# Linear and softmax attention on one core: projections as column tiles, zero products in planned idle time, delayed fills, smaller GpSimd groups

## The chip, the core and the metric

One NeuronCore of a Trainium2 chip runs the whole program. Its engines work side by side and wait for each other through semaphores: TensorE (PE, with its weight loads shown as PEld) multiplies matrices into PSUM, ScalarE (ACT) computes exponentials, VectorE (DVE) does elementwise work and empties PSUM, GpSimd (POOL) does elementwise work between SBUF buffers, and SyncE (SP) issues transfers. Each engine executes its own instructions strictly in the order in which the program lists them. The metric is the device time of one execution in microseconds (us); the time before is the median of three runs.

## The reference

Two attention blocks, A and B, have the same sizes: one sequence of S = 2048 rows, D = 512, H = 32 heads of 16. A is a linear attention, B a full softmax attention. The results are put side by side.

```python
qkv = (x @ wqkv).reshape(B, S, 3, H, Dh).transpose(2, 0, 3, 1, 4)
q, k, v = qkv[0], qkv[1], qkv[2]
# A
phi = lambda t: jnp.where(t > 0, t + 1, jnp.exp(t)) + 1e-6
pq, pk = phi(q), phi(k)
kv = jnp.einsum("bhsd,bhse->bhde", pk, v)
z = jnp.einsum("bhsd->bhd", pk)
o = einsum("bhqd,bhde->bhqe", pq, kv) / (einsum("bhqd,bhd->bhq", pq, z)[..., None] + 1e-6)
# B
scores = jnp.einsum("bhqd,bhkd->bhqk", q, k) * Dh ** -0.5
o = jnp.einsum("bhqk,bhkd->bhqd", softmax(scores), v)
# both
o.transpose(0, 2, 1, 3).reshape(B, S, D) @ wo
```

Nearly all the work is B's: 32 x 2048 x 2048 exponentials. Inputs and outputs are bfloat16.

## The kernel before, in words

**Blocks and units.** B's score matrix is cut into 32 units of 64 blocks. A unit is four heads (one in each group of 32 rows of PE) and 512 queries; a block is 128 keys by 512 queries of one head. `qk` (line 733) makes the scores of a block: K = 32 rows of PE, so up to four blocks of different row groups can run at once. `pv_cand` (line 982) multiplies the exponentials of a block by 17 columns (16 of V and a column of ones) in one of four column groups of PE, and the 48 or more products of a head accumulate in one PSUM bank, `pPV`. When a unit ends, `unit_done` (line 1007) lets DVE transpose that bank, divide, and store into `ON`.

**Two ways to an exponential.** Five PSUM banks (`pS`) form two slots of three and two banks. `fill_act_cand` fills a slot with three or two blocks and ACT computes the exponentials of the whole slot in one operation (line 889). The two `pD` banks serve the other way: DVE turns scores into 16-bit integers whose bits are an approximate exponential in float16 (`DI`, line 829, one block at a time), and GpSimd makes two shifted copies (`DJ`, line 936); the three versions are multiplied by V scaled with three weights, so such a "D block" takes three PV products. A fill may carry D blocks in row groups that its own blocks leave free (`d_pick`, `d_take`, `d_emit`), or `fill_d_cand` makes them alone. D blocks are gathered into groups of `DG` = 3, in `NDG` = 4 group buffers; GpSimd starts on a group when its last block is there (`chain`). `DBL` and `PBL` bound the planned backlog of DVE and GpSimd.

**Projections and block A.** These are jobs of up to 16 products that share the two `pD` banks: `proj_job` (Q and K of B, line 491), `v4_job` (V of B, line 553), `akv_job` (K and V of A, line 590), `aq_job` (Q of A, line 624), `omm_job` (both output projections, line 677), and small ones. `halves` cuts the products of a job into `NPP` = 4 parts, and other work can stand between the parts; the bank stays taken until DVE has emptied it. The products use the full 128 x 128 array. The phi of A takes ACT (line 578) and two bfloat16 operations of DVE (lines 579 and 581).

**The order.** The program is written out by a planner, a loop that keeps a planned clock `T` for each engine. In each step it collects candidates with a planned start and length, drops PE candidates that would let ACT run dry (`keep`), and emits the one that starts first, by priority within 0.03 us. The planned durations are constants: 0.22 us for a fill and for a PV round, 0.216 us for a product of 512 columns, 0.09 + 0.51 us for the integer step of a D block, 0.05 us plus 0.000833 us a column for an exponential. `switch(kind)` adds 0.1 us when PE changes between score products ("q"), PV products ("v") and full-array products ("f"). What the planner fixes is only the order on each engine; on the chip the semaphores decide when an instruction starts.

```python
start = max(T["pe"], t0, afree[sl], ptfree.get((row, sl), 0.0) - 0.5)
dur = switch("q") + 0.22
...
bi = min((i for i in range(ND) if dfree[i] is not None), key=lambda i: (dfree[i], i), default=None)
...
if bi is None or u is None or dfree[bi] > at or d_backlog(at) > DBL or p_backlog(at) > PBL or lagging(at):
    return None
```

The first two lines are of the fill for ACT, the others of `d_pick`: a fill takes a D block along only if a `pD` bank is free when the fill starts.

Of the kernel before, what the change touches and what calls it, by code (L numbers as in the profile page):

```python
# [7 lines left out]
BF = mybir.dt.bfloat16  # L8
# [226 lines left out]
def bass_concat_heads__linear_attn_block__softmax_full_mha__prompt_kernel(nc, A_x, A_wqkv, A_wo, B_x, B_wqkv, B_wo, out):  # L235
# [22 lines left out]
    DBL = 4.0  # L258
    PBL = 4.5
    SHL = ("pool", "pool")  # L260
    TRACE = None


# [7 lines left out]
    with es:  # L271
# [151 lines left out]
        tok = {}  # L423
        seq = [0]

        def push(eng, ready, prio, dur, run):
            seq[0] += 1
            cands[eng].append((ready, prio, seq[0], dur, run))

        class Job:  # L430

# [12 lines left out]
            def stage_done(self, i, end, bk, bi):  # L444
                eng = self.stages[i][0]
                if i == self.rel and bi is not None:
                    dfree[bi] = vis(eng, end)
                for st, tk in self.gives:
                    if st == i:
                        tok[tk] = vis(eng, end)  # L450
                if i + 1 < len(self.stages):
                    eng2, dur, fn = self.stages[i + 1]
                    push(eng2, end if eng2 == eng else vis(eng, end),
                         self.prio if eng2 == "pe" else (0 if eng2 == "act" or (i + 1 <= self.rel and self.bank) else min(self.prio, 2)), dur,
                         lambda st_, en_, fn=fn: (fn(bk), self.stage_done(i + 1, en_, bk, bi)))
# [16 lines left out]
        def halves(fn, reads, n=4, parts=NPP, dur=MM, after=None):  # L472

            def mk(lo, hi):
                def f(e, bk):
                    for i in range(lo, hi):
                        ins = fn(e, bk, i)
                    return ins
                def add(bk):
                    sch.add("pe", lambda e: f(e, bk), reads=reads, writes=[bk[3]], accum=("ch", bk[3], id(fn)))  # L480
                    if after is not None and hi == n:
                        after()
                return add
            w = n // parts
            return [("pe", w * dur, mk(i * w, (i + 1) * w)) for i in range(parts)]
# [2 lines left out]

        def proj_job(Gp, sc, kind, fast=False, **kw):
            def mm(e, bk, cc):  # L490
                return e.matmul(f32v(bk), lhsT=Wb[:, cc, kind * 512 + Gp * 128:kind * 512 + Gp * 128 + 128],  # L491
                                rhs=xTb[:, cc, sc * 512:(sc + 1) * 512], start=(cc == 0), stop=(cc == 3))
            r = Gp % 2
            cs = slice(sc * 512, (sc + 1) * 512)
            i = Gp * NC + sc
            st = halves(mm, [("Wb", kind, Gp)] + [("xTb", t) for t in range(4 * sc, 4 * sc + 4)])
# [87 lines left out]
        def akv_job(t, hp, **kw):  # L584
            n = 4 * hp + t // 4
            c0 = (n % 2) * 512 + (t % 4) * 128
            def mm(e, bk, i):
                k_, cc = divmod(i, 4)
                o_ = f32v(bk)[:, 128:384] if k_ == 0 else f32v(bk).rearrange("p (a n) -> p a n", n=128)[:, 0::3, :]
                return e.matmul(o_, lhsT=xTa[:, cc, c0:c0 + 128],  # L590
                                rhs=Wa[:, cc, 512 + 512 * k_ + 256 * hp:512 + 512 * k_ + 256 * hp + 256], start=(cc == 0), stop=(cc == 3))
# [28 lines left out]
        def aq_job(sc, bq, **kw):  # L620
            n = 8 + sc
            c0 = (n % 2) * 512
            def mm(e, bk, cc):
                return e.matmul(f32v(bk), lhsT=Wa[:, cc, bq * 128:(bq + 1) * 128], rhs=xTa[:, cc, c0:c0 + 512],  # L624
                                start=(cc == 0), stop=(cc == 3))
            st = halves(mm, ["Wa", ("xTa", n % 2)], after=(lambda: next_xa(n)) if bq == 3 else None)
# [46 lines left out]
        def omm_job(ab, t, o2, needs, gives, lane="dve", **kw):  # L673
            WO, wkey, col0 = (WOa, "WaV", 0) if ab == "a" else (WOb, ("Wb", 2), 512)
            def mm(e, bk, hb):
                src = ONT[:, t % 2, hb * 128:(hb + 1) * 128] if ab == "a" else ON[:, 4 * hb + t // 4, (t % 4) * 128:(t % 4 + 1) * 128]
                return e.matmul(f32v(bk), lhsT=src, rhs=WO[:, hb, :], start=(hb == 0), stop=(hb == 3))  # L677
# [5 lines left out]
            return Job(halves(mm, ins_ + [wkey]) + [(lane, 0.6 if lane == "dve" else 0.48, fin)],  # L683
                       needs + [("akv", 1, bl) for bl in range(2)], gives, **kw)


# [156 lines left out]
        def fill_act_cand():  # L843
# [53 lines left out]
        def fill_d_cand():  # L897
# [7 lines left out]
            at = max(at, T["pe"] + d_backlog(T["pe"]) - DBL + 0.01)  # L905
            pk = d_pick(at + 1e-6, ())
            if pk is None:
                return None
# [184 lines left out]
        def job_cand():  # L1093
            best = None
            bi = min((i for i in range(ND) if dfree[i] is not None), key=lambda i: dfree[i], default=None)
            for lst, pr in ((urgent, 0.5), (early, 2), (bjobs, 2.2), (urgent2, 2.3), (ajobs, 2.5)):
                for pos, j_ in enumerate(lst[:1] if lst is not urgent2 else lst[:8]):
# [9 lines left out]
                    if best is None or (st, pr) < (best[0], best[1]):  # L1107
                        def run(st_, en_, j_=j_, lst=lst, fn=fn):
# [6 lines left out]
                        best = (st, pr, eng, dur, run)  # L1115
            return best

        npick = 0
        while True:
            opts = []  # L1120
            for eng in T:
# [5 lines left out]
                        best = (k_, st, c_)  # L1127
                if best is not None:
                    c_ = best[2]
                    opts.append((best[1], c_[1], eng, c_[3] + (switch("f") if eng == "pe" else 0.0), c_[4], c_, "f"))  # L1130
            fa = fill_act_cand()
            if fa is not None:
                opts.append((fa[0], 0, "pe", fa[1], fa[2], None, "q"))
# [7 lines left out]
                opts.append((pc[0], pc[3], "pe", pc[1], pc[2], None, "v"))  # L1141
            jc = job_cand()
            if jc is not None:
                opts.append((jc[0], jc[1], jc[2], jc[3] + (switch("f") if jc[2] == "pe" else 0.0), jc[4], None, "f"))
            if not opts:
                break

# [11 lines left out]
            if eng == "pe":  # L1159
                pk[0] = kind  # L1160
            run_(st, st + dur)
            npick += 1
            if TRACE is not None:
# [3 lines left out]
        if TRACE is not None:  # L1167
            for w in range(0, int(max(T.values())) + 1, 50):
                print(w, {k_: round(sum(max(0, min(b_, w + 50) - max(a_, w)) for a_, b_, e_, _ in TRACE if e_ == k_), 1) for k_ in T}, dgroup["n"])
            print("plan", {k_: round(v_, 1) for k_, v_ in T.items()}, npick,  # L1170
                  {k_: round(sum(b_ - a_ for a_, b_, e_, _ in TRACE if e_ == k_), 1) for k_ in T})

        last = {}
# [77 lines left out]
```

## Time and profile before

| | us |
|---|---|
| runs | 810.81, 813.84, 801.38 (median 810.81) |
| the profiled execution, its time | 817.54 |
| its span, first to last instruction | 815.8 |
| mean granted clock of PE | 0.916 of full speed |

The profile comes from one execution, so durations in the prediction are set against 815.8 us and 817.54 us. A page of it lists the busy time of each engine, a strip of 40 slices of the span, the chain of work that ended last, and the costliest groups of instructions by line. In a group row, "x640 | 738.6, 1349" means 640 instructions, 738.6 us in which at least one of them ran, 1349 ns as the mean of one; what follows is the idle time of the engine just before them and what ended it. Instructions overlap in their pipelines, above all on PE, so a mean is longer than the distance from one to the next. PEclk is the clock that was granted to PE, in tenths of full speed.

Of the chain that ended last, ACT holds 62%, PE 23% and DVE 13%; 60% of the span is the exponential at line 889.

### The profile page before, as it was taken

Reading aid. Unit: us, or ns where it says so; the run is one execution under the profiler, and the core shown is the slowest. Engines: PE = TensorE matmul, PEld = TensorE weight load, DVE = VectorE, ACT = ScalarE, POOL = GpSimd, SP = SyncE. Lnnn points to the kernel's source line nnn. Section 1 sums busy time; section 2 is a strip of 40 time slices with the busy share of each in tenths; the row PEclk is TensorE's granted clock in tenths of the full one; section 3 lists DMA queues with packets and bytes.
Section 4 is the critical chain, followed back from the end, with each engine's and each line's share of the span. In section 5 each row is a group of like instructions: output and inputs, shape, how many; then the busy total and the mean of one; then the engine's idle time right before and its main releaser. Section 6 shows DMA issues by size and latency. Waiting matters only on the chain.

```text
span 815.8 us, 14322 instructions
## 1 busy us (share of the span) xinstructions
PE 726.8 (89%) x6056; PEld 214.7 (26%) x6056; DVE 536.9 (66%) x829; ACT 751.7 (92%) x677; POOL 467.3 (57%) x349
## 2 busy tenths in 40 slices
PE   7989899999988898988999899899888998998986
PEld 4222332222222332322222232222222222222221
DVE  4865766775786666688467666787676556647361
ACT  4989999999998998999988999999998899999894
POOL 3386764554667474546555766545765555639370
PEclk9978999999997998999876999999998689889797
DMA  9400101101101102011001101001100000100000
GB/s 198 113 2 1 27 1 33 40 8 27 28 1 27 27 2 59 7 35 33 14 7 15 26 20 47 7 12 28 27 8 1 7 14 33 33 27 2 10 17 29
DMA packets 54486, 21.43 MB, mean 26 GB/s; under 512 B 45200, under 2 KB 53904, under 8 KB 54416
## 3 DMA queue, kind: packets, MB, share of 16 engines
q1 hardware_dynamic: 53360, 20.20, 11.1%
q8 instruction: 49, 0.80, 0.4%
q10 hardware_dynamic: 1056, 0.26, 0.1%
q14 instruction: 21, 0.17, 0.1%
HBM read 4.19 MB, written 4.19 MB: 10 GB/s over the span
## 4 chain that ended last, share of the span: by engine, by line
ACT 62%; PE 23%; DVE 13%; DMA 1%; SPq 1%; issue 1%; POOL 0%; ACTq 0%
ACT PT L889 60%; PE pPV L982 9%; PE pS L733 7%; DVE DI L829 4%; PE pD L733 2%; DVE PQT L581 2%; DVE KV L581 2%; ACT EA L578 1%; PE pD L677 1%; DVE EA L579 1%; DVE OT L1007 1%; PE pD L624 1%; DMA xTb<-in_B_x_dram 1%; PE pD L590 1%; PE pD L491 1%
## 5 line engine op out<-in xcount | busy, mean ns | idle before, releaser
L889 ACT ACTIVATE PT<-pS 128x1536 f16<-128x1536 f32 (+1 forms) x640 | 738.6, 1349 | 43.7 <-PE pS L733 25.9
L936 POOL TENSOR_SCALAR DJ<-DI 128x1536 int16<-128x1536 int16 x300 | 444.2, 1481 | 319.9 <-DVE DI L829 304.9
L829 DVE TENSOR_SCALAR DI<-pD 128x512 int16<-128x512 f32 (+1 forms) x443 | 301.0, 693 | 160.8 <-PE pD L733 150.1
L733 PE MATMUL pS<-QT,KM 32*128 32x512 bf16 x1599 | 268.0, 411 | 51.0 <-ACT PT L889 43.5
L982 PE MATMUL pPV<-PT,VV 128*17 128x512 f16 x1599 | 268.3, 408 | 0.0
L982 PE MATMUL pPV<-DJ,VV 128*17 128x512 f16 x898 | 193.6, 411 | 0.9 <-POOL DJ L936 0.9
L733 PE MATMUL pD<-QT,KM 32*128 32x512 bf16 x449 | 174.1, 408 | 12.9 <-DVE DI L829 8.2
L733 PEld LDWEIGHTS pS<-QT,KM 32*128 32x128 bf16 x1599 | 61.8, 92 | 253.9 <-ACT PT L889 199.9
L982 PE MATMUL pPV<-DI,VV 128*17 128x512 f16 x449 | 107.6, 417 | 4.5 <-DVE OT L1007 3.3
L982 PEld LDWEIGHTS pPV<-PT,VV 128*17 128x17 bf16 x1599 | 57.4, 88 | 92.2 <-issue 86.9
L982 PEld LDWEIGHTS pPV<-DJ,VV 128*17 128x17 bf16 x898 | 41.4, 89 | 46.9 <-issue 38.2
L733 PEld LDWEIGHTS pD<-QT,KM 32*128 32x128 bf16 x449 | 39.8, 92 | 46.8 <-DVE DI L829 21.2
L590 PE MATMUL pD<-Wa,xTa 128*128 128x256 bf16 x256 | 44.3, 283 | 3.9 <-DVE DI L829 3.6
L1007 DVE STREAM_TRANSPOSE OT<-pPV 128x512 f32<-128x512 f32 x32 | 22.7, 710 | 35.0 <-PE pPV L982 35.0
L491 PE MATMUL pD<-xTb,Wb 128*128 128x512 bf16 x124 | 40.6, 386 | 2.6 <-DMA xTb<-in_B_x_dram 2.0
L469 DVE CAST KV<-pD 128x512 bf16<-128x512 f32 x30 | 20.7, 691 | 23.7 <-PE pD L677 23.4
L982 PEld LDWEIGHTS pPV<-DI,VV 128*17 128x17 bf16 x449 | 22.3, 89 | 31.1 <-issue 17.4
L597 DVE CAST KV<-pD 128x512 bf16<-128x512 f32 x32 | 21.9, 685 | 6.9 <-PE pD L590 6.4
L590 PEld LDWEIGHTS pD<-Wa,xTa 128*128 128x128 bf16 x256 | 18.6, 99 | 26.2 <-issue 16.6
L624 PE MATMUL pD<-xTa,Wa 128*128 128x512 bf16 x64 | 24.2, 424 | 1.1 <-DVE DI L829 1.0
L1013 DVE TENSOR_TENSOR OT<-OT,ZR 128x256 bf16<-128x256 f32 x32 | 24.3, 760 | 0.9
L677 PE MATMUL pD<-Wb,ON 128*128 128x512 bf16 x64 | 22.6, 427 | 2.4 <-DVE ON L1018 2.3
(71 smaller groups left out, 342.7 us busy)
## 6 DMA issues: line engine op xcount, KB each, us to landing
out_dram<-KV SPq DMA_DIRECT2D x32, 128.0 KB, 1.7
KM<-KR SPq DMA_DIRECT2D x96, 16.0 KB, 1.8
Wa<-in_A_wqkv_dram SPq DMA_DIRECT2D x1, 1024.0 KB, 6.0
Wb<-in_B_wqkv_dram SPq DMA_DIRECT2D x2, 384.0 KB, 4.9
Wb<-in_B_wqkv_dram SPq DMA_DIRECT2D x1, 512.0 KB, 4.6
Wa<-in_A_wqkv_dram SPq DMA_DIRECT2D x1, 512.0 KB, 6.8
Wa<-in_A_wo_dram SPq DMA_DIRECT2D x1, 512.0 KB, 5.3
Wb<-in_B_wo_dram SPq DMA_DIRECT2D x1, 512.0 KB, 4.0
```

The lines of the kernel that those rows point to most:

```text
L491: return e.matmul(f32v(bk), lhsT=Wb[:, cc, kind * 512 + Gp * 128:kind * 512 + Gp * 128 + 128], rhs=xTb[:, cc, sc * 512:(sc + 1) * 512], st ...
L581: ("dve", 0.6, f_op("dve", lambda e: e.scalar_tensor_tensor(x, x, 0.0, E, op0=ALU.max, op1=ALU.add), [("EA", q)] + keys, keys))]
L590: return e.matmul(o_, lhsT=xTa[:, cc, c0:c0 + 128], rhs=Wa[:, cc, 512 + 512 * k_ + 256 * hp:512 + 512 * k_ + 256 * hp + 256], start=(cc == ...
L624: return e.matmul(f32v(bk), lhsT=Wa[:, cc, bq * 128:(bq + 1) * 128], rhs=xTa[:, cc, c0:c0 + 512], start=(cc == 0), stop=(cc == 3))
L677: return e.matmul(f32v(bk), lhsT=src, rhs=WO[:, hb, :], start=(hb == 0), stop=(hb == 3))
L733: return e.matmul(dst, lhsT=KM[32 * g:32 * g + 32, Gp % 2, e_, j * 128:(j + 1) * 128], rhs=QT[32 * g:32 * g + 32, Gp % 2, c * 512:(c + 1) ...
L829: sch.add("dve", lambda e: e.tensor_scalar(DI[:, buf, i * 512:(i + n) * 512], DB[:, bi * 512:(bi + n) * 512], ESC, EB, op0=ALU.mult, op1=A ...
L889: sch.add("act", lambda e: e.activation(PT[:, row, c0:c0 + w], SCR[sl][:, 0:w], ACTF.Exp, scale=SC), reads=skeys(sl), writes=[("PT", row, ...
L936: sch.add(ln, lambda e: e.tensor_scalar(J, I, 1.0, float(SH[k]), op0=ALU.mult, op1=ALU.add), reads=[("DI", buf, i) for i in range(n)], wri ...
L982: sch.add("pe", lambda e, g=g, j=j, h=h, k=k, P=P, first=first, last_=last_: e.matmul(PVb[32 * g:32 * g + 17, 0:512], lhsT=VV[:, Gp % 2, k ...
L1007: sch.add("dve", lambda e: e.transpose(OT[:, 0, :], PVb[:, 0:512]), reads=[("PV", g) for g in range(4)], writes=[("OT", 0)])
L1013: ("dve", 0.35, f_op("dve", lambda e: e.tensor_tensor(xn[:, :, 16 * e_:16 * e_ + 16], o[:, :, 0:16], zr.unsqueeze(2).broadcast_to([128, 16 ...
```

## The change

- `mm4` replaces the full-array product in `proj_job`, `akv_job`, `aq_job` and `omm_job`: four products of 32 columns, each at its own column position, which write the four quarters of the same PSUM bank. `v4_job` and the small jobs keep the full array. In the planner these jobs become kind "v", the kind of the PV products, so a change between them and PV costs no `switch`.
- `NPP` goes from 4 to 2: the products of a job are cut into two parts (`v4_job` too).
- `DG` goes from 3 to 2 and `NDG` from 4 to 6.
- A fill for ACT that is not urgent starts later, when a `pD` bank comes free before the latest start at which ACT does not run dry (`late`, with a margin `LATE` = 0.1 us).
- `fill_idle` looks at each PE instruction that the planner starts over 0.25 us after the one before. It puts products of a zero tile `FZ` there, 17 columns by 512, into the PV bank of a unit that still accumulates (adding zero) or into a free `pD` bank, as many as fit and until the planned streaming time of the last `FW` = 3.4 us reaches the share `FU` = 0.7. `LONE` = 0.0 changes nothing.
- DVE clears `FZ` (128 x 512) once at the start.

```diff
-    DG = 3
-    NDG = 4
+    DG = 2
+    NDG = 6
-    NPP = 4
+    NPP = 2
+    FU = 0.7
+    LATE = 0.1
+    LONE = 0.0
+    FW = 3.4
+        FZ = sb("FZ", [128, 512], BF)
+        sch.add("dve", lambda e: e.memset(FZ[:], 0.0), writes=["FZ"])
...
+        def mm4(e, out, lhsT, rhs, start, stop):
+            for g in range(4):
+                ins = e.matmul(out[32 * g:32 * g + 32], lhsT=lhsT[:, 32 * g:32 * g + 32], rhs=rhs, start=start, stop=stop, tile_position=(0, 32 * g))
+            return ins
...
             def mm(e, bk, cc):
-                return e.matmul(f32v(bk), lhsT=Wb[:, cc, kind * 512 + Gp * 128:kind * 512 + Gp * 128 + 128],
-                                rhs=xTb[:, cc, sc * 512:(sc + 1) * 512], start=(cc == 0), stop=(cc == 3))
+                return mm4(e, f32v(bk), Wb[:, cc, kind * 512 + Gp * 128:kind * 512 + Gp * 128 + 128],
+                           xTb[:, cc, sc * 512:(sc + 1) * 512], cc == 0, cc == 3)
...
-            st = halves(mm, ["Wa", "WaV", ("xTa", n % 2)], n=8, parts=NPP, dur=0.11, after=after if t % 4 == 3 else None)
+            st = halves(mm, ["Wa", "WaV", ("xTa", n % 2)], n=8, parts=NPP, dur=0.11, after=after if t % 4 == 3 else None, kind="v")
...
             dur = switch("q") + 0.22
+            late = T["act"] + sum(exps) - dur - TAIL["pe"] - SEM - LATE
+            if nfill[0] >= NS and start < late:
+                fr = sorted(x for x in dfree if x is not None)[:4 - len(bl)]
+                for x in fr:
+                    if start < x <= late:
+                        start = x
...
+        streams = []
+        def fill_idle(st, kind):
+            a, b = T["pe"], st - 0.05
+            u = pvu[0]
+            gs = [] if u >= NU or pvopen[0] is None else [g for g in range(4) if not pv_first[u][g] and tleft[u][g] > 0]
+            bi = min((i for i in range(ND) if dfree[i] is not None and dfree[i] <= a), key=lambda i: dfree[i], default=None)
+            if not gs and bi is None:
+                return 0
+            lo = st - FW
+            while streams and streams[0][1] <= lo - 5.0:
+                streams.pop(0)
+            need = FU * FW - sum(max(0.0, min(y, st) - max(x, lo)) for x, y in streams)
+            a += switch("v")
+            n = min(int((b - (0.0 if kind == "v" else 0.1) - a) / 0.216), int(need / 0.216 + 0.999))
+            if n <= 0:
+                return 0
+            g = gs[0] if gs else 0
+            dst = PVb if gs else f32v(DBANK[bi])
+            def f(e):
+                for _ in range(n):
+                    ins = e.matmul(dst[32 * g:32 * g + 17, 0:512], lhsT=FZ[:, 0:17], rhs=FZ[:], start=not gs, stop=not gs, tile_position=(0, 32 * g))
+                return ins
...
+            pk[0] = "v"
+            return n
...
+            if eng == "pe":
+                if st - T["pe"] > 0.25:
+                    s0 = switch(kind)
+                    k_ = fill_idle(st, kind)
+                    nz += k_
+                    dur += switch(kind) - s0
+                streams.append((st + switch(kind), st + dur))
+                pk[0] = kind
             T[eng] = st + dur
```

More of the change, by code (lines that the diff above doesn't have):

```diff
@@ L424, in bass_concat_heads__linear_attn_block__softmax_full_mha__prompt_kernel, with push @@
         seq = [0]
-        def push(eng, ready, prio, dur, run):
+        def push(eng, ready, prio, dur, run, kind="f"):
             seq[0] += 1
-            cands[eng].append((ready, prio, seq[0], dur, run))
+            cands[eng].append((ready, prio, seq[0], dur, run, kind))
         class Job:
@@ L466, in bass_concat_heads__linear_attn_block__softmax_full_mha__prompt_kernel, with halves @@
         MM = 0.216
+        def mm4(e, out, lhsT, rhs, start, stop):
+            for g in range(4):
+                ins = e.matmul(out[32 * g:32 * g + 32], lhsT=lhsT[:, 32 * g:32 * g + 32], rhs=rhs, start=start, stop=stop, tile_position=(0, 32 * g))
+            return ins
         def copy_to(lane, out_fn, in_fn):
             return lambda e, bk: (e.tensor_copy(out_fn(), in_fn(bk)) if lane == "dve" else e.activation(out_fn(), in_fn(bk), ACTF.Copy))
-        def halves(fn, reads, n=4, parts=NPP, dur=MM, after=None):
+        def halves(fn, reads, n=4, parts=NPP, dur=MM, after=None, kind="f"):
             def mk(lo, hi):
@@ L495, in proj_job @@
             i = Gp * NC + sc
-            st = halves(mm, [("Wb", kind, Gp)] + [("xTb", t) for t in range(4 * sc, 4 * sc + 4)])
+            st = halves(mm, [("Wb", kind, Gp)] + [("xTb", t) for t in range(4 * sc, 4 * sc + 4)], kind="v")
             needs = [("xTb", t) for t in range(4 * sc, 4 * sc + 4)]
@@ L589, in mm @@
                 o_ = f32v(bk)[:, 128:384] if k_ == 0 else f32v(bk).rearrange("p (a n) -> p a n", n=128)[:, 0::3, :]
-                return e.matmul(o_, lhsT=xTa[:, cc, c0:c0 + 128],
-                                rhs=Wa[:, cc, 512 + 512 * k_ + 256 * hp:512 + 512 * k_ + 256 * hp + 256], start=(cc == 0), stop=(cc == 3))
+                return mm4(e, o_, xTa[:, cc, c0:c0 + 128], Wa[:, cc, 512 + 512 * k_ + 256 * hp:512 + 512 * k_ + 256 * hp + 256], cc == 0, cc == 3)
             def after():
@@ L623, in mm @@
             def mm(e, bk, cc):
-                return e.matmul(f32v(bk), lhsT=Wa[:, cc, bq * 128:(bq + 1) * 128], rhs=xTa[:, cc, c0:c0 + 512],
-                                start=(cc == 0), stop=(cc == 3))
-            st = halves(mm, ["Wa", ("xTa", n % 2)], after=(lambda: next_xa(n)) if bq == 3 else None)
+                return mm4(e, f32v(bk), Wa[:, cc, bq * 128:(bq + 1) * 128], xTa[:, cc, c0:c0 + 512], cc == 0, cc == 3)
+            st = halves(mm, ["Wa", ("xTa", n % 2)], after=(lambda: next_xa(n)) if bq == 3 else None, kind="v")
             st.append(("dve", 0.6, f_ev("dve", lambda e, bk: e.tensor_copy(PQT[:, 0, bq, :], f32v(bk)), [], [("PQT", 0, bq)])))
@@ L1114, in run @@
                             j_.stage_done(0, en_, bk, b_)
-                        best = (st, pr, eng, dur, run)
+                        best = (st, pr, eng, dur, run, getattr(fn, "kind", "f"))
             return best
-        npick = 0
+        streams = []
[20 more added lines that the diff above has]
+                return ins
+            if gs:
+                sch.add("pe", f, reads=["FZ"], writes=[("PV", g)], accum=("pv", u, g))
+            else:
+                sch.add("pe", f, reads=["FZ"], writes=[DBANK[bi][3]])
+            for i in range(n):
+                streams.append((a + 0.216 * i, a + 0.216 * (i + 1)))
+            pk[0] = "v"
+            return n
+        npick = nz = 0
         while True:
@@ L1143, in bass_concat_heads__linear_attn_block__softmax_full_mha__prompt_kernel @@
             if jc is not None:
[L1144 removed]
+                opts.append((jc[0], jc[1], jc[2], jc[3] + (switch(jc[5]) if jc[2] == "pe" else 0.0), jc[4], None, jc[5]))
             if not opts:
@@ L1169, in bass_concat_heads__linear_attn_block__softmax_full_mha__prompt_kernel @@
                 print(w, {k_: round(sum(max(0, min(b_, w + 50) - max(a_, w)) for a_, b_, e_, _ in TRACE if e_ == k_), 1) for k_ in T}, dgroup["n"])
-            print("plan", {k_: round(v_, 1) for k_, v_ in T.items()}, npick,
+            print("plan", nz, {k_: round(v_, 1) for k_, v_ in T.items()}, npick,
                   {k_: round(sum(b_ - a_ for a_, b_, e_, _ in TRACE if e_ == k_), 1) for k_ in T})
```

13 lines of the change are left out of this document (6 added, 7 removed).

## The prediction

> **What bounds the kernel now.** I read the page's first two parts, then its groups, then windows cut at the changes of the granted clock, then the timeline just before one such change.
>
> ```profile
> span 815.8 us, 14322 instructions
> ...
> PE 726.8 (89%) x6056; PEld 214.7 (26%) x6056; DVE 536.9 (66%) x829; ACT 751.7 (92%) x677; POOL 467.3 (57%) x349
> ...
> PEclk9978999999997998999876999999998689889797
> ```
>
> ScalarE (ACT) is nearest to its limit: 64.1 us of the span are not its own work. The clock row is not all nines: 13 stretches between 20 and 800 us ran at half clock. The next two fences are sums of windows between 20 and 800 us: first the stretches at full clock, then those at half clock; the columns are length, busy time of PE, PEld, DVE, ACT and POOL.
>
> ```profile
> sum 657.10, PE 584.23 PEld 180.03 DVE 459.99 ACT 645.46 POOL 384.53; mean PE 41.73 PEld 12.86 DVE 32.86 ACT 46.10 POOL 27.47
> ```
> ```profile
> 626.00:646.50 20.50, 19.65 (x119) 4.09 (x123) 11.17 (x17) 14.15 (x14) 9.14 (x6) 0.50 0.00 0
> ...
> sum 123.00, PE 119.13 PEld 23.70 DVE 63.85 ACT 92.79 POOL 75.41; mean PE 9.16 PEld 1.82 DVE 4.91 ACT 7.14 POOL 5.80
> ```
>
> ACT is idle 657.10 - 645.46 = 11.6 us at full clock (1.8%), 123.00 - 92.79 = 30.2 us at half clock (25%) and the other 22.3 us of the 64.1 lie in head and tail. So at full clock ACT is the bound, and nothing that only relieves PE helps there; at half clock PE is the bound (97% busy). What starts a half-clock stretch? The sum below is over eight of the 3.4 us windows just before one; under it is the timeline at one of them (start, length).
>
> ```profile
> 622.60:626.00 3.40, 1.70 (x10) 0.43 (x10) 3.37 (x3) 3.40 (x4) 2.50 (x2) 1.00 0.02 5
> ...
> sum 27.20, PE 15.49 PEld 4.33 DVE 22.42 ACT 27.20 POOL 15.62; mean PE 1.94 PEld 0.54 DVE 2.80 ACT 3.40 POOL 1.95
> ```
> ```profile
> 620.61 4.57 POOL L936 TENSOR_SCALAR DJ<-DI 128x1536 int16<-128x1536 int16 x3
> ```
> ```profile
> 622.42 1.36 DVE L579 TENSOR_SCALAR EA<-EA 128x512 bf16<-128x512 bf16 x1
> 623.81 1.91 DVE L581 SCALAR_TENSOR_TENSOR PQT<-PQT,EA 128x512 bf16<-128x512 bf16 x1
> ```
> ```profile
> 624.10 0.39 PE L733 MATMUL pS<-QT,KM 32*128 32x512 bf16 x3 [0.19 <-ACT PT L889]
> 626.38 0.60 PE L733 MATMUL pD<-QT,KM 32*128 32x512 bf16 x1 [1.89 <-DVE DI L829]
> ```
>
> In those windows PE's row is 57% busy (15.49 of 27.20) against 89% at full clock, and DVE's 82%. In the example two bf16 operations of DVE last 1.36 and 1.91 us beside three back-to-back GpSimd operations, PE stands 1.89 us behind a D bank, and the clock halves for 20.5 us. The same line at its shortest and longest:
>
> ```profile
> L581 DVE SCALAR_TENSOR_TENSOR PQT<-PQT,EA x16: 680/1060/1909, 350.8 to 632.8; 128x512 bf16<-128x512 bf16 x16
> ```
>
> The Trainium skill ("TensorE: Matmul & The Clock Gate", Part 1) has PE go to half clock after an idle window of about 3.4 us and warns of idle gaps over about 3 us. No such gap stands in these rows, where 1.70 of 3.40 us are busy; here a half-busy window was enough, and the measurement decides.
>
> **Part by part.** The groups that carry the prices:
>
> ```profile
> L889 ACT ACTIVATE PT<-pS 128x1536 f16<-128x1536 f32 (+1 forms) x640 | 738.6, 1349 | 43.7 <-PE pS L733 25.9
> L936 POOL TENSOR_SCALAR DJ<-DI 128x1536 int16<-128x1536 int16 x300 | 444.2, 1481 | 319.9 <-DVE DI L829 304.9
> L829 DVE TENSOR_SCALAR DI<-pD 128x512 int16<-128x512 f32 (+1 forms) x443 | 301.0, 693 | 160.8 <-PE pD L733 150.1
> L733 PE MATMUL pS<-QT,KM 32*128 32x512 bf16 x1599 | 268.0, 411 | 51.0 <-ACT PT L889 43.5
> L733 PE MATMUL pD<-QT,KM 32*128 32x512 bf16 x449 | 174.1, 408 | 12.9 <-DVE DI L829 8.2
> L590 PE MATMUL pD<-Wa,xTa 128*128 128x256 bf16 x256 | 44.3, 283 | 3.9 <-DVE DI L829 3.6
> ```
>
> *Column tiles.* 576 full-array products (128 at line 491, 256 at 590, 64 at 624, 128 at 677, from the loops) become 2304 of 32 columns, with as many weight loads. Do four tiles run at once, and what does a change of array shape cost?
>
> ```profile
> 305.21 1.05 PE L590 MATMUL pD<-Wa,xTa 128*128 128x256 bf16 x8
> ```
> ```profile
> 310.19 0.39 PE L982 MATMUL pPV<-PT,VV 128*17 128x512 f16 x2
> 310.50 0.39 PE L590 MATMUL pD<-Wa,xTa 128*128 128x256 bf16 x2
> ```
> ```profile
> 313.78 0.59 PE L982 MATMUL pPV<-DJ,VV 128*17 128x512 f16 x3
> 314.00 0.38 PE L982 MATMUL pPV<-PT,VV 128*17 128x512 f16 x2
> 314.22 0.38 PE L982 MATMUL pPV<-DI,VV 128*17 128x512 f16 x1
> ```
> ```profile
> 364.62 0.56 PE L636 MATMUL pD<-RHA,PQT 128*128 128x8 bf16 x16
> ```
>
> PV rounds of column tiles follow every 0.22 us (313.78, 314.00, 314.22), so a projection round of 512 keeps its price; the far end, four in a row, is 0.86. A round of 256 costs (1.05 - 0.283)/7 = 0.11 us now; 16 load-and-product pairs took 0.56 us, 0.035 each, so four pairs may need 0.14: up to 256 x 0.03 = +8 us on PE; I take 0, by the PV rows. PV to projection is 0.31 us from start to start (310.19 to 310.50), 0.09 to 0.10 over a round: that is the switch that goes. Its count:
>
> ```profile
> PEld pD L677 <- issue: 23.0, 80, 1.0
> PEld pD L491 <- issue: 16.8, 61, 2.2
> PEld pD L590 <- issue: 16.6, 67, 0.4
> PEld pD L624 <- issue: 10.8, 38, 0.4
> ```
>
> 246 entries x 0.1 = 25 us of PE; parts per job fall from four to two (448 to 224 in 112 jobs), at most 22 us more. I take 30. In time it is worth what it saves at half clock (counted below) and some of the 11.6 us of ACT's idle time at full clock: bounds 0 and 11.6, taken 3, near 0 because ACT is busy 98% there. A part of two products is coarser to fit before a fill; that is the lower bound below nothing, +5.
>
> The Trainium skill ("TensorEngine Tiling (Array Packing)", Gotcha 2) says that column tiling excludes the fast weight load. With "TensorE: Matmul & The Clock Gate", LDWEIGHTS, where a load takes its columns over 1.2 GHz, four loads of 32 columns are an estimated 0.107 us, as long as a round of 256; not hidden, that would be 27 us on PE and eat the 30. No run here shows such loads.
>
> *Zero products.* They stand in planned idle stretches over 0.25 us, until streams fill 0.7 of the last 3.4 us. PE's row is idle 815.8 - 726.8 = 89 us, so at most some 410 products of 0.216 us, hidden by that idle time; where PE really runs late they cost up to their length. They write the PV bank or a free D bank, so a zero product also waits if DVE is behind the plan. Their worth is the clock. Without any half-clock stretch ACT's idle time there would fall from 30.2 us to 1.8% of 123, 2.2 us: gain between 0 and 28.0. I take two thirds, 18.7: the windows before a stretch lack about a third of PE's usual work, which two or three products make up, but a PE held behind a D bank issues no product either.
>
> *Groups of two.* 449 blocks need 225 groups, 450 operations.
>
> ```profile
> L936 POOL TENSOR_SCALAR DJ<-DI 128x1024 int16<-128x1024 int16 x2 | 2.1, 1044 | 0.2
> ```
>
> 450 x 1.044 = 470 us against 444.2: +26 us, hidden by POOL's 319.9 us of waiting. The longest stretch that line 581 can be held beside one operation falls from 1.48 to 1.04 us; that supports the two thirds and isn't counted again. Twelve block buffers stay twelve.
>
> *Fills wait for D banks.* A ScalarE fill may be put off, up to 0.1 us before ACT would run dry, until a D bank comes free, so that a D block rides in its unused row groups. The 640 fills have at most 640 x 4 - 1599 = 961 free places; 449 D blocks exist, so at least 191 fills carry none. One block moved from ACT to DVE saves 738.6/1599 = 0.462 us of ACT and costs 0.69 us of DVE and 1.04 us of POOL. Bounds: no growth, 0; DVE at 90% of a 780 us span, (702 - 537)/0.69 = 240 blocks, -111 us. Only the two-block fills have room to wait, since they are refilled during the longer three-block ACT operation: half of 191, and less than half of the time a bank comes free in that room, so 38 blocks, nearer to nothing. 38 x 0.462 = -17.6 us. Behind a put-off fill stand the PV rounds and projection parts on PE; they are planned into the wait. Afterwards ACT is still last.
>
> Sum: 815.8 - 18.7 - 17.6 - 3.0 = 776.5 us of span, +1.7 around it (the profiled execution took 817.54) = 778.2. The median shown, 810.81, is 0.992 of that execution: 772 us.
>
> **The rivals.**
> *The zero products don't hold the clock*: a product of 17 columns uses a small part of the array and may not count. Then 815.8 - 17.6 - 3.0 + 1.7 = 796.9, times 0.992 = 790. Against it: at 57% busy the clock fell, at 89% it held, and most of that busy time is of products that use a quarter of the array each. By the idle-window rule of the Trainium skill ("TensorE: Matmul & The Clock Gate", Part 1) these products would have nothing to prevent, as no idle window of 3.4 us stands in the rows.
> *D blocks grow by a hundred*, because fewer, shorter job parts free banks and PE: 815.8 - 18.7 - 46.2 - 3.0 + 1.7 = 749.6, 744. For it: DVE and POOL are idle 34% and 43%.
> *Nothing arrives*: fills find no bank in time and the clock stays: 800 to 815.
> *PE held at D banks (slower).* The plan gives an eviction 0.60 us, the row 0.69, so banks come late just where fills now aim.
>
> ```profile
> PEld pD L733 <- DVE DI L829: 21.2, 43, 2.2
> ```
>
> That is 21.2/449 = 0.05 us a block. PE's cover is 89 + 30 less zero products in two thirds of the 89 us (60), 59 us; over 487 blocks it is used up from 0.17 us a block. At 0.2 and with twice the half-clock time: 815.8 + (97 - 21 - 59 = 17) + 28 - 17.6 + 1.7 = 845, 838 in the median. Against it: the score product for ACT stands ahead of the D product in each fill, so ACT has one fill in hand.
>
> **How the numbers follow.** Forecast 0.45; clock not held 0.20; many D blocks 0.15; nothing 0.10; held at D banks 0.10. About 2% is what the runs (801.38 to 813.84) can tell, so faster means under 795: the first, the third and most of the second, 0.75; same 0.15; slower 0.10. The range leaves out the slower case and the far half of the D case: 742 to 804. The likeliest case alone spans 755 to 788.
>
> **What would show it.** Clock row: nearly all nines, under 50 us at half clock; otherwise the zero products failed. pS under 1599 and pD near 487, with fewer lone pD rounds; otherwise the waits found no bank. POOL operations of 1024 near 1.04 us and line 581 no longer near 1.9. Projection rounds of four tiles at 0.22 us and no 0.1 us gap after PV; a longer pitch would mean that loads aren't hidden. The wait of pD for DI above 60 us, or ACT idle over 2% at full clock, would make the forecast wrong from the side of the D banks.

## The result and the profile after

The changed kernel takes 766.2 us (median of four runs, 762.40 to 771.96) against 810.71 us (a fourth run of the kernel before is counted in): the ratio is 0.9475, with a 95% interval of 0.943 to 0.952. The profiled execution took 767.73 us, with a span of 765.8 us, so the two profiles differ by 50.0 us of span. The medians differ by 44.5 us only: the profiled execution of the kernel before, 817.54 us, is longer than each of its four runs (801.38 to 813.84). Medians and ratios are of fast executions; this matters in experiment 10 alone, where three of ten lie over 1.5% above the fastest and are left out.

The page of the changed kernel, cut as before:

```profile
span 765.8 us, 18359 instructions
...
PE 696.7 (91%) x7975; PEld 225.5 (29%) x7975; DVE 541.7 (71%) x858; ACT 732.2 (96%) x664; POOL 535.0 (70%) x529
...
PEclk9998999999989979999999899999999999999999
...
ACT 75%; PE 13%; DVE 9%; DMA 1%; POOL 1%; issue 0%; ACTq 0%
...
L905 ACT ACTIVATE PT<-pS 128x1536 f16<-128x1536 f32 x627 | 719.3, 1388 | 15.6 <-PE pS L743 9.8
L952 POOL TENSOR_SCALAR DJ<-DI 128x1024 int16<-128x1024 int16 x480 | 511.2, 1065 | 204.8 <-DVE DI L839 174.7
...
L743 PE MATMUL pS<-QT,KM 32*128 32x512 bf16 x1568 | 250.8, 393 | 44.3 <-ACT PT L905 37.3
...
L743 PE MATMUL pD<-QT,KM 32*128 32x512 bf16 x480 | 177.2, 393 | 8.5 <-DVE DI L839 5.4
...
L1155 PE MATMUL pPV<-FZ 128*17 128x512 bf16 x115 | 43.3, 400 | 0.0
```

ACT's share of the chain that ended last went from 62 to 75%, PE's from 23 to 13%. Line 905 is the exponential (889 before), 743 the scores (733), 998 the PV products (982), 952 the GpSimd copies (936), 839 the integer step (829), 593 the last addition of phi (581), 476 the column tiles, and 1155 the zero products: 115 into the PV bank and 14 more into D banks. There are 480 D blocks against 449.

The same two sums of windows as in the prediction, at full clock and then at half clock, each from 20 us to 16 us before the end:

```profile
sum 688.80, PE 629.64 PEld 203.46 DVE 505.49 ACT 683.53 POOL 491.54; mean PE 89.95 PEld 29.07 DVE 72.21 ACT 97.65 POOL 70.22
...
sum 41.00, PE 40.88 PEld 10.08 DVE 21.61 ACT 31.45 POOL 33.57; mean PE 6.81 PEld 1.68 DVE 3.60 ACT 5.24 POOL 5.59
```

Read ACT's idle time as length less ACT: 5.3 us at full clock (11.6 before) and 9.6 us at half clock (30.2 before), whose length fell from 123 to 41 us. Head and tail hold 18.7 us (22.3 before). With 751.7 - 732.2 = 19.5 us less work on ACT the bill is 19.5 + 20.6 + 6.3 + 3.6 = 50.0 us, the whole difference of the spans. The time at half clock differs from one execution to the next: the mean granted clock of the four runs is 0.960 to 0.979. Half-clock times of 41 and 50 us in two profiles are therefore not told apart.

### The profile page after: what moved, and what is told of

The parts are those of the page before. It is cut to its first block, busy times and chain, and to the rows that moved or that the text cites. A ratio compares the mean times of both kernels' runs of the same rounds, so it can differ in the third digit from the quotient of the medians.

```text
span 765.8 us, 18359 instructions
## 1 busy us (share of the span) xinstructions
PE 696.7 (91%) x7975; PEld 225.5 (29%) x7975; DVE 541.7 (71%) x858; ACT 732.2 (96%) x664; POOL 535.0 (70%) x529
## 3 DMA queue, kind: packets, MB, share of 16 engines
q1 hardware_dynamic: 53360, 20.20, 11.6%
## 4 chain that ended last, share of the span: by engine, by line
ACT 75%; PE 13%; DVE 9%; DMA 1%; POOL 1%; issue 0%; ACTq 0%
ACT PT L905 74%; PE pPV L998 4%; PE pS L743 4%; DVE DI L839 3%; PE pD L476 3%; PE pD L743 2%; ACT EA L590 1%; DVE EA L591 1%; DVE KV L593 1%; DMA xTb<-in_B_x_dram 1%; POOL DJ L952 1%; DVE PQT L593 1%; DVE OT L1023 1%; DVE OT L1029 1%; PE pPV L1155 1%
## 5 line engine op out<-in xcount | busy, mean ns | idle before, releaser
L905 ACT ACTIVATE PT<-pS 128x1536 f16<-128x1536 f32 x627 | 719.3, 1388 | 15.6 <-PE pS L743 9.8
L952 POOL TENSOR_SCALAR DJ<-DI 128x1024 int16<-128x1024 int16 x480 | 511.2, 1065 | 204.8 <-DVE DI L839 174.7
L839 DVE TENSOR_SCALAR DI<-pD 128x512 int16<-128x512 f32 x471 | 318.1, 694 | 108.4 <-PE pD L743 94.8
L743 PE MATMUL pS<-QT,KM 32*128 32x512 bf16 x1568 | 250.8, 393 | 44.3 <-ACT PT L905 37.3
L998 PE MATMUL pPV<-PT,VV 128*17 128x512 f16 x1568 | 253.9, 392 | 0.5 <-ACT PT L905 0.3
L743 PEld LDWEIGHTS pD<-QT,KM 32*128 32x128 bf16 x480 | 41.7, 91 | 46.5 <-DVE DI L839 26.6
L476 PE MATMUL pD<-Wa,xTa 128*32 128x256 bf16 x1024 | 44.1, 280 | 1.2 <-DVE DI L839 1.0
L1155 PE MATMUL pPV<-FZ 128*17 128x512 bf16 x115 | 43.3, 400 | 0.0
L476 PE MATMUL pD<-xTb,Wb 128*32 128x512 bf16 x496 | 42.1, 393 | 0.9 <-DVE DI L839 0.7
L480 DVE CAST KV<-pD 128x512 bf16<-128x512 f32 x30 | 20.6, 686 | 18.7 <-PE pD L476 18.5
L476 PEld LDWEIGHTS pD<-Wa,xTa 128*32 128x32 bf16 x1024 | 27.1, 97 | 11.2 <-DVE DI L839 4.8
L576 POOL TENSOR_SCALAR VV<-VV 128x544 bf16<-128x544 bf16 x24 | 16.6, 690 | 7.2 <-DVE VV L572 6.2
```

Source lines behind the costliest of these rows:

```text
L476: ins = e.matmul(out[32 * g:32 * g + 32], lhsT=lhsT[:, 32 * g:32 * g + 32], rhs=rhs, start=start, stop=stop, tile_position=(0, 32 * g))
L576: st.append((lane, 0.25 if lane == "dve" else 0.65, f_op(lane, lambda e, k=k: e.tensor_scalar(vv(k), vv(0), SW[k], 0.0, op0=ALU.mult, op1= ...
L743: return e.matmul(dst, lhsT=KM[32 * g:32 * g + 32, Gp % 2, e_, j * 128:(j + 1) * 128], rhs=QT[32 * g:32 * g + 32, Gp % 2, c * 512:(c + 1) ...
L839: sch.add("dve", lambda e: e.tensor_scalar(DI[:, buf, i * 512:(i + n) * 512], DB[:, bi * 512:(bi + n) * 512], ESC, EB, op0=ALU.mult, op1=A ...
L905: sch.add("act", lambda e: e.activation(PT[:, row, c0:c0 + w], SCR[sl][:, 0:w], ACTF.Exp, scale=SC), reads=skeys(sl), writes=[("PT", row, ...
L952: sch.add(ln, lambda e: e.tensor_scalar(J, I, 1.0, float(SH[k]), op0=ALU.mult, op1=ALU.add), reads=[("DI", buf, i) for i in range(n)], wri ...
```

## The experiments

Each starts from the changed kernel unless it says otherwise. "Replanned" means that the planner made another order for it; "same order" means that every engine keeps the changed kernel's order. Ratios are to the kernel before. A replanned order also has its own number of zero products: 132, 125, 110, 146, 119 and 114 in experiments 2, 3, 4, 8, 11 and 12, against 129 in the changed kernel.

**1. No zero products, replanned.**

```diff
-    FU = 0.7
+    FU = 0.0
```

> The changed kernel without its 129 zero products (FU = 0); the order is planned anew and holds 475 D blocks against 480. Theory (the zero products hold the clock): half-clock time between head and tail goes from 41 us back to 90 to 130 us, ACT's idle time there from 9.6 to 22 to 30 us; with 5 blocks more on ACT (2.3 us) the time is 779 to 791 us, ratio to before 0.962 to 0.975. Rival (the shorter GpSimd operations and the freed PE time hold it): half-clock time stays under 60 us, time 765 to 772, ratio 0.944 to 0.952.

793.4 us, ratio 0.981 (0.972 to 0.990), with 117.3 us at half clock. The clock fell as the theory has it, but the time is over its upper end. The kernel of experiment 9 separates the two causes.

**2. Full-array projections, replanned.**

```diff
-            for g in range(4):
-                ins = e.matmul(out[32 * g:32 * g + 32], lhsT=lhsT[:, 32 * g:32 * g + 32], rhs=rhs, start=start, stop=stop, tile_position=(0, 32 * g))
-            return ins
+            return e.matmul(out, lhsT=lhsT, rhs=rhs, start=start, stop=stop)
...
-kind="v")
+kind="f")
```

> The changed kernel with full-array products in the four projection jobs, planned as their own shape again; 470 D blocks against 480. Theory (the column tiles save a 0.1 us change of array shape at some hundred places, which is worth time only through D blocks and slack): 10 blocks more on ACT are 4.6 us, ACT's idle time grows by 3 to 10 us: 774 to 781 us, ratio 0.955 to 0.964. Rival (tiles are worth the whole gain, 4 % or more): over 795. Rival (tiles are worth nothing): 763 to 770.

790.3 us, ratio 0.980 (0.971 to 0.988): more than expected. The sums of windows of this kernel, full clock and half clock, show that it isn't the clock:

```profile
sum 714.80, PE 645.12 PEld 197.48 DVE 507.07 ACT 696.46 POOL 492.30; mean PE 107.52 PEld 32.91 DVE 84.51 ACT 116.08 POOL 82.05
...
sum 34.10, PE 33.58 PEld 6.12 DVE 16.18 ACT 27.19 POOL 21.70; mean PE 6.71 PEld 1.22 DVE 3.23 ACT 5.44 POOL 4.34
```

Half clock is 34.1 us, but ACT idles 18.3 us at full clock. Experiment 7 asks whether the chip or the order did that.

**3. Groups of three, replanned.**

```diff
-    DG = 2
-    NDG = 6
+    DG = 3
+    NDG = 4
```

> The changed kernel with groups of three blocks in four buffers; 477 D blocks. Theory (DVE's bf16 operations wait out a GpSimd operation, so its length sets the longest PE stall): the longest STT of DVE goes from 1.52 back to about 1.9 us, half-clock time from 41 to 50 to 80 us, ACT idle 3 to 8 us more, 3 blocks more on ACT 1.4 us: 770 to 776 us, ratio 0.950 to 0.957. Rival (group size doesn't matter): 763 to 769, half-clock time as in the changed kernel. Rival (fewer, longer operations are better): under 762.

777.1 us, ratio 0.962 (0.953 to 0.971), over the theory's end. In windows, full clock and half clock:

```profile
sum 692.60, PE 623.22 PEld 198.90 DVE 517.77 ACT 680.97 POOL 457.51; mean PE 62.32 PEld 19.89 DVE 51.78 ACT 68.10 POOL 45.75
...
sum 44.40, PE 43.27 PEld 10.78 DVE 21.10 ACT 34.74 POOL 28.27; mean PE 4.81 PEld 1.20 DVE 2.34 ACT 3.86 POOL 3.14
```

The half-clock time is nearly the changed kernel's (44.4 against 41.0 us); ACT idles 11.6 us at full clock against 5.3. These 6.3 us are most of the 7.2 us between the spans of the two profiles (773.0 and 765.8 us). So the shorter GpSimd operation doesn't show in the clock, where the theory and the prediction put it, but in ACT's waits at full clock.

**4. Fills don't wait, replanned.**

```diff
-    LATE = 0.1
+    LATE = 1e9
```

> The changed kernel whose fills no longer wait for a D bank. The prediction gave the waits 38 more D blocks and 17.6 us. The program planned without them still holds 479 D blocks, 142 of them in rounds of their own against 116, so the prediction's reading would need 17 us from elsewhere. Theory now (D blocks come from freed PE time and banks, waits only move them into fills): about 30 more PE rounds with two changes of shape, some 10 us of PE, ACT idle 0 to 5 us more: 765 to 773 us, ratio 0.944 to 0.953. Rival (waits are worth what was forecast): 778 to 786.

777.1 us, ratio 0.961 (0.954 to 0.969), half clock 48.0 us, ACT idle 10.0 us at full clock. The time is over the theory's end and under the rival's. The D blocks stay (479), so they aren't what the waits give. Where the 10.9 us come from isn't shown: the order is another one, and it has 19 zero products fewer.

**5 and 6. What about a zero product holds the clock? Same order.** Fewer rows, or fewer columns:

```diff
-lhsT=FZ[:, 0:17], rhs=FZ[:], start=not gs
+lhsT=FZ[0:32, 0:17], rhs=FZ[0:32, :], start=not gs
```

> The changed kernel, order and number of instructions untouched, but its 129 zero products stream 32 rows of the zero tile in place of 128. In the traces so far, the share of the four row groups of PE that stream, averaged over a 3.41 us window, was at most 0.385 in the windows just before a half-clock stretch and, with four exceptions in some 800 windows, above that in the others. Theory (the clock follows that share, so a product of 128 rows counts in full and one of 32 rows a quarter): the clock falls about as often as without zero products: half-clock time 80 to 120 us against 41, 780 to 795 us, ratio 0.962 to 0.980. Rival (any streaming product counts in full): half-clock time under 60 us, 763 to 771 us. Rival (what helped was the new order and not the clock): 763 to 771 us with a low clock.

```diff
-dst[32 * g:32 * g + 17, 0:512], lhsT=FZ[:, 0:17]
+dst[32 * g:32 * g + 1, 0:512], lhsT=FZ[:, 0:1]
```

> The changed kernel, order untouched, but its zero products have one column in place of 17, still 128 rows. Theory (rows count, columns don't): as the changed kernel, half-clock time 25 to 60 us, 762 to 771 us, ratio 0.940 to 0.952. Rival (the part of the array in use counts): the clock falls as without zero products, 780 to 795 us.

The sums at half clock, with 32 rows and with one column:

```profile
sum 71.60, PE 70.89 PEld 16.55 DVE 35.73 ACT 53.53 POOL 50.18; mean PE 7.88 PEld 1.84 DVE 3.97 ACT 5.95 POOL 5.58
```
```profile
sum 51.30, PE 51.21 PEld 10.80 DVE 25.24 ACT 39.36 POOL 38.04; mean PE 6.40 PEld 1.35 DVE 3.15 ACT 4.92 POOL 4.75
```

With 32 rows: 778.8 us, ratio 0.960 (0.954 to 0.967), 71.6 us at half clock; both lie below the theory's ranges (780 and 80), and far from the first rival. With one column: 767.3 us, 0.947 (0.940 to 0.954), 51.3 us, as the theory has it. Both keep the order and the number of instructions. Rows count for the clock; how many columns a product has does not show.

**7. Full-array projections, same order.** The first diff of experiment 2 alone, with kind "v" kept.

> The changed kernel with the order of its four tiles kept, but each projection product full-array again: 480 D blocks, 129 zero products, the same instruction order, only the four tiles of a product are one instruction. Theory (what the tiles give is the 0.1 us change of array shape on the chip): the trace of the changed kernel has 197 borders between PV and projection rounds, 20 us of PE come back, most of them late for ACT since PE has little slack left: ACT idle at full clock 13 to 22 us against 5.3, 774 to 786 us, ratio 0.955 to 0.970. Rival (the loss without tiles came from the planner's other order): 763 to 770 us.

772.9 us, ratio 0.9545 (0.9485 to 0.9606), below the theory's range, and the interval overlaps the changed kernel's. ACT idles 7.2 us at full clock, where the theory has 13 to 22. With the order kept, giving up the tiles costs some 6.7 us; the other 17 us of experiment 2 came with the planner's other order.

**8. The planner takes DVE's time as measured, replanned.**

```diff
-push("dve", vis("pe", en), 0, 0.09 + 0.51 * n, p1)
+push("dve", vis("pe", en), 0, 0.16 + 0.53 * n, p1)
```

> The changed kernel whose planner takes 0.16 + 0.53 us for a block, near the 0.69 us that DVE needs, in place of 0.09 + 0.51; 472 D blocks against 480, 91 of them in rounds of their own against 116. Theory (the stalls of PE behind D banks are small by now, 32 us in all, and mostly hidden): 8 blocks more on ACT are 3.7 us, so 766 to 773 us, ratio 0.945 to 0.955. Rival (PE held at D banks is what is left of ACT's idle time and of the half-clock stretches): half-clock time under 25 us, 755 to 763 us.

766.6 us, ratio 0.947 (0.941 to 0.953): the theory's time, with the rival's half clock of 14.4 us. ACT idles 7.6 us less at half clock than in the changed kernel, but it has 3.4 us more work (735.6) and idles 2.4 us more at full clock (7.6), and the medians are equal. The waits of PE for the integer step fell (17.4 against 32.0 us), but there are also 17 zero products more, so it isn't shown which of the two holds the clock.

**9. Zero products left out, same order.**

```diff
-            if gs:
-                sch.add("pe", f, reads=["FZ"], writes=[("PV", g)], accum=("pv", u, g))
-            else:
-                sch.add("pe", f, reads=["FZ"], writes=[DBANK[bi][3]])
```

> The changed kernel with its order kept, but the 129 zero products are not issued. It parts the two things that came with taking them out by replanning (793 us): the clock and the planner's other order. Theory (the clock is most of it): half-clock time 75 to 130 us against 41, 779 to 792 us, ratio 0.960 to 0.978. Rival (the other order cost most of the 27 us): 766 to 775 us.

779.0 us, ratio 0.962 (0.957 to 0.967). In windows, full clock and half clock:

```profile
sum 646.40, PE 573.13 PEld 187.51 DVE 474.19 ACT 639.34 POOL 443.53; mean PE 44.09 PEld 14.42 DVE 36.48 ACT 49.18 POOL 34.12
...
sum 95.50, PE 93.68 PEld 22.29 DVE 51.25 ACT 77.85 POOL 79.24; mean PE 7.81 PEld 1.86 DVE 4.27 ACT 6.49 POOL 6.60
```

So 129 products shorten the half-clock time from 95.5 to 41.0 us and are worth 779.0 - 766.2 = 12.8 us. (The granted clock agrees in all runs: 0.933 to 0.938 without them, 0.950 to 0.956 with 32 rows, 0.960 to 0.979 with all.) The other 14 us of experiment 1 came with its order.

**10. Column tiles alone, on the kernel before (replanned).** The edit to the four jobs, with `DG` 3, `NDG` 4, `NPP` 4, no waits and no zero products.

> The kernel before with column tiles in the four projection jobs as its only edit (groups of three, four parts, no waits, no zero products): 457 D blocks against 449. Theory (tiles free PE time, which alone is worth little because the clock falls as before): ACT 3.7 us less, half-clock time 90 to 140 us, 798 to 809 us, ratio 0.984 to 1.0. Rival (tiles are the largest part by themselves): under 790 us.

814.0 us (median of seven), ratio 1.002 (0.997 to 1.007), over the theory's end: alone they give nothing, with 131.1 us at half clock.

**11. Groups of one.**

```diff
-    DG = 2
-    NDG = 6
+    DG = 1
+    NDG = 12
```

> The changed kernel with groups of one block in twelve buffers: 487 D blocks, 974 GpSimd operations. From 1.481 us for three blocks and 1.065 for two, one block should take about 0.65 us, so GpSimd is busy some 630 us against 511. Theory (the longest DVE operation follows the length of one GpSimd operation): the longest STT falls from 1.52 to about 1.35 us, the half-clock time doesn't rise, ACT 3.2 us less: 758 to 768 us, ratio 0.935 to 0.950. Rival (GpSimd becomes late and PV waits for its copies): 772 us or more, with waits of PV products on DJ over 25 us against 7.

786.4 us, ratio 0.973 (0.967 to 0.979): the rival. The waits of this kernel (total, times, longest) and its window sums:

```profile
PEld pPV L998 <- POOL DJ L952: 50.2, 87, 2.0
PE pPV L998 <- POOL DJ L952: 21.9, 38, 1.5
```
```profile
sum 725.30, PE 651.41 PEld 210.34 DVE 509.40 ACT 697.47 POOL 608.59; mean PE 93.06 PEld 30.05 DVE 72.77 ACT 99.64 POOL 86.94
...
sum 20.50, PE 20.50 PEld 5.69 DVE 10.18 ACT 15.40 POOL 18.02; mean PE 3.42 PEld 0.95 DVE 1.70 ACT 2.57 POOL 3.00
```

GpSimd is busy 608.6 of 725.3 us, PV products wait for its copies and hold PE, and ACT idles 27.8 us although the half-clock time is only 20.5 us. Of the three lengths, each with its own order, two blocks is the best: three hold DVE longer, one makes GpSimd late.

**12. More D blocks, replanned.** `DLEAD` is how long before the end of DVE's planned work a D block may be made in a round of its own.

```diff
-    DLEAD = 0.5
-    LATE = 0.1
+    DLEAD = 0.8
+    LATE = 0.05
```

> The changed kernel with two planner constants moved (DLEAD 0.8 for 0.5, LATE 0.05 for 0.1), which makes 488 D blocks and 114 zero products. Theory (ACT is the bound, so each block moved is worth 0.46 us): 3.7 us less ACT, 758 to 766 us, ratio 0.935 to 0.947. Rival (fewer zero products and later fills give it back): 766 to 774 us with more than 60 us at half clock.

763.6 us, ratio 0.942 (0.937 to 0.948), with 488 D blocks, 44.3 us at half clock and 730.3 us of ACT. It is the lowest median, but its interval overlaps that of the changed kernel, so it isn't shown to be faster.

## Why the prediction was right

**The bound.** ACT at full clock and PE at half clock, as read: the bill above closes by those three parts with head and tail. Forecast and measured: half-clock idle time 18.7 and 20.6 us, ACT's work 17.6 and 19.5, full-clock idle time 3.0 and 6.3, head and tail nothing and 3.6; together 39.3 and 50.0 us of span. What was forecast as two thirds of the half-clock time is two thirds (123 to 41).

**The zero products** were given all of the 18.7 us. Same order, they are worth 12.8: the step is mis-sized. By the window sums it is more so: ACT's idle time at half clock is 30.2 us before, 17.7 in experiment 9 without zero products, and 9.6 with them. So 8.1 of the 20.6 us are theirs, and 12.5 came with the other edits in this order; which of them brought these isn't shown (tiles alone leave 31.1), and some may belong to the long execution profiled before. Leaving the zero products out also adds 2.5 us to ACT's work and 1.8 us to its idle time at full clock. Nor are there two or three in each weak window: 129 in all, where 410 was the bound.

**The D blocks** came, 480 against 487 forecast, but the step that led there failed: it has the waiting fills add 38 blocks, and without any wait there are still 479. That the number came out near is luck. No single edit is shown to bring them: 470 are left without tiles, 475 without zero products, 477 with groups of three, and tiles alone make 457; the two-part jobs were not taken out alone. What the waits do is to take D blocks into fills: of the emitted orders, the one with waits has 116 blocks in rounds of their own, the one without has 142. The kernel before has 111, so the sign "fewer lone pD rounds" did not come. The 11 us of the waits (experiment 4) were measured with a replanned order, so how much is theirs on the chip stays open.

**The tiles.** A round follows 0.22 us after the start of a PV round and the 0.1 us gap is gone; two rows of the timeline of the changed kernel, where it was 0.31 before:

```profile
310.76 0.39 PE L998 MATMUL pPV<-PT,VV 128*17 128x512 f16 x2
310.98 0.60 PE L476 MATMUL pD<-xTb,Wb 128*32 128x512 bf16 x8
```

Do the four loads of 32 columns hold up a round of 256? The same view, one part of four rounds:

```profile
306.51 0.65 PE L476 MATMUL pD<-Wa,xTa 128*32 128x256 bf16 x16
```

With 0.28 us for the last, (0.65 - 0.28)/3 = 0.12 us a round; from start to start, over all such rounds of a part, the median is 0.11 us in both kernels. So the loads are hidden. The 27 us that the prediction estimated from the Trainium skill's load time ("TensorE: Matmul & The Clock Gate", LDWEIGHTS) are not there. The value put on them, 3 us, lies under the 6.7 of experiment 7, whose interval doesn't exclude it. Replanned, their loss costs 24 us, and alone they give nothing: there is no one price for this edit.

**Groups of two** were priced at nothing beside the clock. Experiment 3 gives 10.9 us, at nearly the same half-clock time: a missing term, of ACT's waits at full clock. The mechanism in the prediction was right (line 593 at its longest: 1.52 us, 1.91 with groups of three), its place was not. ACT's 11.6 us of idle time at full clock before, of which the prediction gave 3.0 to the tiles, are back with groups of three. That kernel was replanned too, so some of the 10.9 us may be its order.

**The rivals.** The clock was held. PE behind D banks, the slower rival, grew little; the waits of the D product for DVE in the changed kernel:

```profile
PEld pD L743 <- DVE DI L839: 26.6, 66, 1.6
...
PE pD L743 <- DVE DI L839: 5.4, 12, 1.3
```

By the first row, the one that the prediction used, 26.6 us over 480 blocks are 0.06 us each, against 0.05 before and the 0.17 from which it was to decide. Where the time comes out near the forecast, part of it is luck, errors that met: the zero products were put too high, and groups of two, and what the other edits do at half clock, at nothing. Nor does the median show how much too small the sum was, 39.3 of 50.0 us of span, since the profile before was of a long execution.

## What to carry to other kernels

Cut the trace at the changes of the granted clock and make the bill in each part by the engine that bounds it: tiles alone, which are to free PE, gave nothing in a kernel whose ACT was 98% busy at full clock. Where a planner writes the order, taking out one edit also reshuffles everything: the zero products were worth 27 us replanned and 13 us in a fixed order, the same tiles 24 and 7; keep the order and swap the instruction if the price on the chip is wanted. Edits that feed on each other have no separate shares: the four losses (27, 24, 11 and 11 us) add up to more than the 44.5 us that all brought.

## What the runs showed of the hardware

**PE's clock follows the share of its row groups that stream.** The half-clock stretches last 3.4 us or a multiple, so I cut the full-clock time between head and tail of the 14 traces into windows of 3.41 us. For each, from all product records, I computed four shares of the window: any product streaming; the row groups streaming (a product of 128 rows counts 1, one of 32 rows a quarter); the column groups streaming; and the array area. A drop is a window after which the clock halved. The best single threshold of each, fitted to these same windows:

```
129 drops, 2529 other windows
share          threshold   drops above it   others below it   errors
any product    0.445       71               10                81
row groups     0.373        7                8                15
column groups  0.348      100               13               113
array area     0.327       32               50                82
```

Row groups separate best by far, and experiments 5 and 6 bear it out on the chip: zeros over 128 rows hold the clock with 17 columns or one. Over 32 rows they hold it in part (71.6 us at half clock, against 95.5 without and 41.0 with all rows) and give no time over leaving them out (778.8 against 779.0 us). The Trainium skill ("TensorE: Matmul & The Clock Gate", Part 1) has the clock fall after an idle window of about 3.4 us; in these traces 71 of the 129 drops came after windows in which some product streamed over 0.445 of the time, and the measurement decides. That zeros count shows in the same runs. Whether 0.373 holds for other kernels no run here shows.

**A DVE operation waits out one GpSimd operation.** The addition of line 593 (two SBUF inputs) and the length of GpSimd's operations (shortest, median, longest, in ns), in groups of two, three and one:

```profile
L593 DVE SCALAR_TENSOR_TENSOR KV<-KV,EA x16: 675/1109/1516, 80.6 to 322.0; 128x512 bf16<-128x512 bf16 x16
...
L952 POOL TENSOR_SCALAR DJ<-DI x480: 1047/1047/1487, 15.8 to 747.2; 128x1024 int16<-128x1024 int16 x160
```
```profile
L593 DVE SCALAR_TENSOR_TENSOR KV<-KV,EA x16: 676/693/1909, 75.6 to 322.4; 128x512 bf16<-128x512 bf16 x16
...
L952 POOL TENSOR_SCALAR DJ<-DI x318: 1471/1472/1847, 14.5 to 753.5; 128x1536 int16<-128x1536 int16 x159
```
```profile
L593 DVE SCALAR_TENSOR_TENSOR KV<-KV,EA x16: 675/1022/1058, 77.0 to 323.1; 128x512 bf16<-128x512 bf16 x16
...
L952 POOL TENSOR_SCALAR DJ<-DI x974: 617/619/1136, 13.1 to 763.6; 128x512 int16<-128x512 int16 x195
```

The longest is the median GpSimd operation plus 0.47, 0.44 and 0.44 us; the shortest, 0.68 us, is the same in all three. That it is a wait shows in the ends. Of the 128 such additions in these three traces and the one before, 81 start while a GpSimd operation runs. Of these, 77 end 0.53 to 0.54 us after that operation's end; the other four, where it had at most 0.12 us left, take 0.67 to 0.68 us. The 47 that start beside none take 0.67 to 0.69 us. The Trainium skill ("GPSIMD Engine Reference", Key points) names DVE instructions with two SBUF inputs, and those in a two-port mode, as the ones that contend with GpSimd; the rows agree for this line and add the length of the hold.
